# Graph aggregation on one core: broadcast buffers from a pool of their own, and smaller merge credits between the decoding's steps

## Chip, core and metric

One core of a Trainium2 chip. The time is the device time of one launch in microseconds (us). The kernel before was timed three times: 1854.63, 1863.13 and 1864.98 us, median 1863.13. One further execution, of 1856.37 us, was profiled; every row quoted here comes from it. Engines are named as in the profile: PE multiplies matrices (PEld loads its weights), DVE is VectorE, ACT is ScalarE, POOL is GpSimd, SP is SyncE, which only issues transfers here.

## What is computed

A mean over neighbours in a graph of 12,500 nodes with 64 features each and 800,000 edges drawn at random, and two small products:

```
nsum    = segment_sum(x[src], dst, N)      # 800,000 rows of 64 added by destination
h_neigh = nsum * deg_inv[:, None]
out     = x @ w_self + h_neigh @ w_neigh
```

The edges come in no order. The whole difficulty is to add 800,000 gathered rows by destination.

## The kernel before

**From edges to buckets.** Each edge becomes one 32-bit key, in which the destination block (82 nodes per half, two halves to a block, 77 blocks) stands above the source block (128 nodes, 98 blocks), and the places within the blocks stand in the lowest bits. A pair of blocks is a *bucket*, or a column; there are 77 x 98 = 7546. The keys are sorted in 128 partitions, cut by value into three *parts* of 29, 20 and 10 buckets per partition (columns 0 to 3711, 3712 to 6271, and the rest), exchanged between partitions through DRAM, and merged. Each part goes through a first set of merges (16 runs to 1), a row split (`split_rows`, with a store to DRAM and eight gathers back by POOL, line 565), a second set of merges (8 runs to 1), and a *decode*. The merges are tensor_tensor minimum and maximum instructions of VectorE (lines 316, 328, and 362 for the last merge of the first part), with a few copies by ScalarE (line 312).

**The decode of a part** (`decode_buckets`). POOL gathers for every bucket a window of keys around it into `v` (lines 736 and 742). In groups of four buckets VectorE splits the keys (`split`, lines 782 and 784), ScalarE narrows them to bf16 (`narrow`, lines 791, 792, 796), the source places are stored to the DRAM list `sl` (line 794, for the first part by SyncE), and the destination places are turned by PE (`turn`, line 802) into `dlT`. After the last group VectorE searches the margins of all windows for keys that did not fit their bucket, the *leftovers* (`beyond` and `pieces`, lines 831, 834 and 860), in `v` and a scratch tile `e`.

**The tile loop** (`nodes`). Columns are worked in tiles of eight, 950 of them. For each chunk of 28 columns `one_hots` broadcasts the source places from `sl` to all partitions (`slb`, line 933: four transfers of 224 KB on SyncE's queue, three buffers), compares them with the partition number (`ohs`, line 935, VectorE), and compares `dlT` with a row of numbers (`ohd`, line 940, VectorE). The loop keeps 44 columns of one-hots ahead of the tile. PE picks the feature rows out of SBUF with `ohs` (line 966), ScalarE copies them to 16 bit (`xg`, line 976), and PE adds them into the destination blocks with `ohd` (line 1047). After every six destination blocks (73.5 tiles) the sums are multiplied by the weights, scaled and added to the output in DRAM by POOL (line 1123). Leftovers are fetched row by row by POOL (`lx`, line 997) and added with one-hots of their own (lines 1006 and 1015).

**The order of the work** is written out by hand: from `after_sort` on, each engine runs its instructions in the order in which the Python code emits them. In that order the merges of parts 1 and 2 fill VectorE beside the decode of the first part and beside the tile loop. A merge instruction yields a charge in ns (`n2 * n / 0.96 + 125`). Between two decoding steps of the first part `t` is raised by a credit, and merges are emitted until it is used up:

```
for i, k in enumerate(self.decode_buckets(0, self.v, vp, mps)):
    t += 1400 if i < 4 else 2800
    if k < KPRS[0]:
        t = fill(t) if t > 0 else t
```

There are 16 such steps, two to a group; the merges behind the last of them come before the search. In the tile loop each tile gives a credit of `PACE[min(merging, 2)] - self.spent`, where `spent` counts VectorE's other extra work and `merging` is 1 until the second merges of part 1 are through, and then 2 and 3. Part 1's decode begins when its second merges are through, and must end 12 tiles before its first column is due; the same holds for part 2. When part 2's decode is through (`changed`), VectorE takes a share of ScalarE's copies.

**Memory.** Tiles come from pools, which are stacked from the left and from the right end of SBUF. `v`, `e` and the decode's small tiles lie in the pool `va`, the first part's merge buffers in `first_two`. Both are closed after the decode, and the tile loop's pool `fin` is then opened from the right; `slb`, `ohs`, `ohd`, `xg` and the leftovers' tiles are in `fin`. An instruction that writes a tile waits until what lay in the same memory has been read.

Of the kernel before, what the change touches and what calls it, by code (L numbers as in the profile page):

```python
# [13 lines left out]
BF = mybir.dt.bfloat16  # L14
# [34 lines left out]
NSUP = 128 // SUP  # L49
LENA = [l[3:] for l in LENS]  # L50
LENB = [l[4:] for l in LENS]
PACE = (0, 420, 405)
LROW = [l[-1] for l in LENS]
LEAD = 616
EXT = 36
# [318 lines left out]
class Kernel:  # L374
# [549 lines left out]
    def one_hots(self, pool):  # L924


        nc = self.nc
        for c in range(0, NBID, 28):
            n = min(28, NBID - c)
            b = pool.tile([128, 28 * 128], BF, name="slb", bufs=3)[:, :n * 128]  # L930
            src = self.sl[c:c + n]
            for j in range(4):
                nc.sync.dma_start(b[j::4], bass.AP(tensor=src.tensor, offset=src.offset, ap=[[0, 32], [1, n * 128]]))  # L933
            s = pool.tile([128, 28, 128], FH, name="ohs", bufs=3)[:, :n]
            nc.vector.tensor_scalar(s.rearrange("p c s -> p (c s)"), b, self.pidx[:, :1], None, op0=OP.is_equal)  # L935
            d = pool.tile([128, 14, HN, 2], FH, name="ohd", bufs=4)[:, :n // 2]
            at = c % TURN
            wide = [128, n // 2, HN, 2]
            ix = self.dlT[:, at:at + n].rearrange("p (c t) -> p c t", t=2)[:, :, None, :].to_broadcast(wide)
            nc.vector.tensor_tensor(d, self.iota[:, None].to_broadcast(wide), ix, op=OP.is_equal)  # L940
            yield [(s[:, j], d[:, j // 2, :, j % 2]) for j in range(n)]
# [345 lines left out]
    def sums_and_merge(self, es, mps, aps, x, u1, u2, u3, runs, first_two, va, vp, counts, merge):  # L1287
        tc = self.tc

        def fill(t):  # L1290
            while t > 0:
                dt = next(merge, None)
                if dt is None:
                    return 0
                t -= dt
            return t

        while counts:
            fill(1)
            for _ in range(2):  # L1300
                if counts and next(counts, None) is None:
                    counts = None
        fill(BEHIND)
        self.gather_buckets(0, NFIRST, KPRS[0])
        t = 0
        for i, k in enumerate(self.decode_buckets(0, self.v, vp, mps)):
            t += 1400 if i < 4 else 2800
            if k < KPRS[0]:
                t = fill(t) if t > 0 else t
        va.close()  # L1310
        first_two.close()


        self.late = True
        self.fin = fin = es.enter_context(tc.tile_pool(name="fin", bufs=1, side="right"))
        self.left = {}
        self.picked = -9
        self.mps = mps
        self.spent = 0
        side = [[self.leftovers(0), 0]]  # L1320
        chain = None
        part, merging = 0, 1
        work = ExitStack()
        last = None
        t = 0
        home = {1: (u1, x, u1), 2: (u2, u1, u2)}
        todo = [(merge, None)]
        given, checked = 0, False

        def split(part, n):  # L1330
            u, w, pong = home[part]
            for wait in self.split_rows(part, u, w, mps, self.nc.gpsimd):
                yield wait
            todo.append((self.merge_runs(LENB[part], w, pong, SUP), part))

        for n in self.nodes(fin, aps, mps):
            for job in list(side):
                if n >= job[1]:
                    wait = next(job[0], None)
                    if wait is None:  # L1340
                        side.remove(job)
                        if len(self.left) == NP and not checked:
                            checked = True
                            side.append([self.check(fin, mps), 0])
                    else:
                        job[1] = n + wait
            if chain is None and part + 1 < merging:
                part += 1
                vp = work.enter_context(tc.tile_pool(name=f"v{part}", bufs=1))
                chain = self.change(part, vp, mps)  # L1350
                last = None
            if chain:
                if last != "gather" or not n % 2 and self.picked < n - 1:
                    last = next(chain, None)
                    if last is None:
                        assert n < BASE[part] // 8 - 12
                        chain = None
                        self.changed = part == NP - 1
                        work.close()
                        side.append([self.leftovers(part), n + 3])  # L1360
            t += PACE[min(merging, 2)] - self.spent
            self.spent = 0
            while t > 0 and todo:
                dt = next(todo[-1][0], None)
                if dt is not None:
                    t -= dt
                    continue
                rows = todo.pop()[1]
                if rows:
                    self.rows[rows] = home[rows][1]  # L1370
                    merging += 1
                else:
                    given += 1
                    assert given == 1 or merging == 2
                    side.append([split(given, n), n + 6])
                    if given == 1:
                        todo.append((self.merge_runs(LENA[2], u2, u3, NSUP), None))
            if not todo:
                t = min(t, 0)
        assert checked  # L1380
        for job, _ in side:
            for _ in job:
                pass
        assert merging == 3 and part == 2 and not chain
        runs.close()
# [27 lines left out]
```

## Time and profile before

| | |
|---|---|
| timed runs | 1854.63, 1863.13, 1864.98 us |
| profiled execution | 1856.37 us, span 1854.6 us |
| busy over the span | PE 986.6 us, DVE 1718.2, ACT 1116.7, POOL 576.2 |
| last merge round of the first part starts | 685.7 us |
| decode of the first part | 737 to 787 us |
| search for leftovers | 787 to 797 us |
| first one-hot of the tile loop | 803.41 us |
| second merges of part 1 through | 1168 us |
| first merges of part 2 through | 1420 us |
| second merges of part 2 through | 1572 us |

A row of the timeline gives the start, the busy time, the engine, the line, the operation, output and inputs, the number of instructions that were merged into the row and, in brackets, the idle time of the engine before it with what ended it. "SPq" is the time at which SyncE's queue issues a transfer; the transfer itself lands later. A row of a group ends with the number of instructions, their busy time and the mean of one in ns, and the idle time ahead of them. The engines' shares over the whole span say little here, since the sort, the decode and the tile loop have different limits: stretches are read instead.

### The profile page before, as it was taken

Reading aid. Unit: us, or ns where it says so; the run is one execution under the profiler, and the core shown is the slowest. Engines: PE = TensorE matmul, PEld = TensorE weight load, DVE = VectorE, ACT = ScalarE, POOL = GpSimd, SP = SyncE. Lnnn points to the kernel's source line nnn. Section 1 sums busy time; section 2 is a strip of 40 time slices with the busy share of each in tenths; the row PEclk is TensorE's granted clock in tenths of the full one; section 3 lists DMA queues with packets and bytes.
Section 4 is the critical chain, followed back from the end, with each engine's and each line's share of the span. In section 5 each row is a group of like instructions: output and inputs, shape, how many; then the busy total and the mean of one; then the engine's idle time right before and its main releaser. Section 6 shows DMA issues by size and latency. Waiting matters only on the chain.

```text
span 1854.6 us, 54153 instructions
## 1 busy us (share of the span) xinstructions
PE 986.6 (53%) x23413; PEld 851.9 (46%) x23413; DVE 1718.2 (93%) x1718; ACT 1116.7 (60%) x1587; POOL 576.2 (31%) x447
## 2 busy tenths in 40 slices
PE   3046000000000000058979979897898899888996
PEld 1015000000000000057868868776887788777885
DVE  6999999999999999989989999998898799978885
ACT  5263000113001005458979989899999899977885
POOL 2000000055502005404456535473332523532331
PEclk7567555555555555579989999999999999999998
DMA  5207100021002002169978888996889788977894
GB/s 174 54 0 169 39 0 0 38 79 51 18 4 73 10 0 82 47 216 266 274 249 253 251 248 254 296 282 227 264 250 284 234 265 242 326 200 257 274 268 118
DMA packets 176789, 307.79 MB, mean 166 GB/s; under 512 B 127885, under 2 KB 133596, under 8 KB 175772
## 3 DMA queue, kind: packets, MB, share of 16 engines
q1 hardware_dynamic: 98268, 275.58, 44.9%
q0 software_dynamic: 78272, 28.65, 9.6%
q8 instruction: 185, 3.03, 0.7%
q14 instruction: 64, 0.52, 0.1%
HBM read 277.01 MB, written 26.52 MB: 164 GB/s over the span
## 4 chain that ended last, share of the span: by engine, by line
DVE 19%; PE 13%; DMA 11%; issue 10%; SPq 5%; POOL 4%; ACT 4%; DVEq 0%; POOLq 0%; ACTq 0%
DMA slb<-sl 10%; PE ct L966 7%; DVE u L328 7%; PE acc L1047 5%; SPq L933 5%; DVE ohs L935 4%; DVE ohd L940 3%; ACT xg L976 2%; DVE u L362 2%; POOL u L565 1%; POOL lx L997 1%; POOL out L1123 1%; DVE u L316 1%; DMA sl<-l 1%; PE acc L1015 1%
## 5 line engine op out<-in xcount | busy, mean ns | idle before, releaser
L976 ACT ACTIVATE xg<-ct 128x1024 f16<-128x1024 f32 x919 | 862.6, 1074 | 104.4 <-PE ct L966 80.0
L966 PE MATMUL ct<-xh,ohs 128*128 128x128 f16 x7546 | 532.6, 224 | 87.9 <-DVE ohs L935 23.7
L966 PEld LDWEIGHTS <-ohs 128*128 128x128 f16 x7546 | 451.8, 100 | 125.4 <-issue 52.5
L328 DVE TENSOR_TENSOR u<-u 128x1512 f32<-128x1512 f32 (+57 forms) x316 | 425.7, 1362 | 12.9 <-ACT u L312 8.6
L1047 PE MATMUL acc<-ohd,xg 64*128 64x82 f16 x15092 | 395.2, 201 | 47.7 <-ACT xg L976 20.4
L1047 PEld LDWEIGHTS <-xg 64*128 64x128 f16 x15092 | 324.6, 96 | 104.6 <-issue 29.2
L997 POOL DMA_INDIRECT lx<-xt,ls x127 | 232.0, 1826 | 425.6 <-PE acc L1015 352.5
L940 DVE TENSOR_TENSOR ohd<-iota,dlT 128x2296 f16<-128x2296 bf16 x270 | 362.2, 1341 | 0.0
L935 DVE TENSOR_SCALAR ohs<-slb,pidx 128x3584 f16<-128x3584 bf16 x270 | 321.8, 1192 | 40.2 <-DMA slb<-sl 19.0
L509 PE MATMUL stp<-cx,swapa 128*128 128x16 f32 (+1 forms) x12 | 3.1, 335 | 398.0 <-DVE swapa L505 398.0
L260 DVE TENSOR_TENSOR a<-b 128x1040 f32<-128x1040 f32 (+41 forms) x130 | 194.7, 1539 | 3.5 <-DVE b L260 0.5
L260 DVE TENSOR_TENSOR b<-a 128x1040 f32<-128x1040 f32 (+46 forms) x150 | 194.6, 1345 | 3.2 <-ACT a L262 0.4
L538 POOL DMA_INDIRECT u<-d,ixa x48 | 72.5, 1511 | 390.8 <-ACT junka L526 335.4
L509 PEld LDWEIGHTS stp<-cx,swapa 128*128 128x128 f32 x12 | 2.6, 271 | 398.5 <-DVE swapa L505 398.5
L312 ACT ACTIVATE u<-u 128x256 f32<-128x256 f32 (+14 forms) x60 | 33.0, 618 | 170.6 <-DVE u L316 134.8
L1123 POOL DMA_DIRECT2D out<-o x27 | 99.1, 3800 | 103.1 <-ACT o L1117 89.8
L802 PE MATMUL tr<-idb,l 128*128 128x128 bf16 x59 | 7.6, 263 | 188.9 <-ACT l L796 188.9
L262 ACT ACTIVATE b<-a 128x2 f32<-128x2 f32 (+31 forms) x41 | 15.9, 402 | 127.1 <-DVE a L260 120.4
L802 PEld LDWEIGHTS <-l 128*128 128x128 bf16 x59 | 4.3, 114 | 191.2 <-ACT l L796 190.8
L316 DVE TENSOR_TENSOR u<-u 128x2016 f32<-128x2016 f32 (+11 forms) x40 | 61.9, 1563 | 16.2 <-DMA u<-da,ixb 8.8
L262 ACT ACTIVATE a<-b 128x1 f32<-128x1 f32 (+24 forms) x34 | 8.6, 259 | 105.4 <-DVE b L260 99.9
L565 POOL DMA_INDIRECT u<-da,ixb x24 | 36.9, 1539 | 88.6 <-ACT ixb L513 85.0
(158 smaller groups left out, 839.4 us busy)
## 6 DMA issues: line engine op xcount, KB each, us to landing
slb<-sl SPq DMA_DIRECT2D x1076, 224.0 KB
xt<-xh SPq DMA_DIRECT2D x1, 3136.0 KB
out<-o POOLq DMA_DIRECT2D x25, 123.0 KB
own<-os SPq DMA_DIRECT2D x12, 256.0 KB
out<-os SPq DMA_DIRECT2D x12, 256.0 KB
rd<-dst SPq DMA_DIRECT2D x5, 512.0 KB
rs<-src SPq DMA_DIRECT2D x5, 512.0 KB
lx<-xt,ls POOLq DMA_INDIRECT x127
```

Of the source, the lines that this page charges most:

```text
L260: nc.vector.tensor_tensor(view(dst, lo + sh, [[st, g], [1, l]]), x, y, op=op)
L316: nc.vector.tensor_tensor(at(oth, to, n), x, y, op=op)
L328: nc.vector.tensor_tensor(to, at(cur, ln + lo, n), at(cur, lo + k, n), op=op)
L538: nc.gpsimd.indirect_dma_start(out=u[:, i * w:(i + 1) * w], out_offset=None, in_=src, in_offset=bass.IndirectOffsetOnAxis(ap=self.start[pa ...
L933: nc.sync.dma_start(b[j::4], bass.AP(tensor=src.tensor, offset=src.offset, ap=[[0, 32], [1, n * 128]]))
L935: nc.vector.tensor_scalar(s.rearrange("p c s -> p (c s)"), b, self.pidx[:, :1], None, op0=OP.is_equal)
L940: nc.vector.tensor_tensor(d, self.iota[:, None].to_broadcast(wide), ix, op=OP.is_equal)
L966: nc.tensor.matmul(ct[:, i * 128:(i + 1) * 128], cols[i][0], self.xh[:, (b0 + i) % NB].rearrange("p a f -> p (a f)"), start=True, stop=True)
L976: nc.scalar.activation(xg[:, :cnt * 128], ct[:, :cnt * 128], AF.Copy)
L997: nc.gpsimd.indirect_dma_start(out=x, out_offset=None, in_=self.xt, in_offset=bass.IndirectOffsetOnAxis(ap=self.left[p][1][:, c:c + 1].bit ...
L1047: nc.tensor.matmul(acc[h][:, db % OCT * HN:(db % OCT + 1) * HN], xg[r, i * 128:(i + 1) * 128], d[r], start=db % OCT == 0 and sb == 0, stop ...
L1123: nc.gpsimd.dma_start(out, o[:n, at], accum_op=OP.add)
```

## The change

`slb` is allocated from a pool `wait`, which is opened from the right before the first part's decode is emitted, while `va` and `first_two` are still open; it stays open to the end. The tile loop's pool is opened further in by as much as `wait` takes. The code that issues the broadcasts stays at its place in the order. From the fifth decoding step on the credit is 1700 instead of 2800. The tile loop's credits are 450 instead of 420 while part 1 is merged, and 420 instead of 405 after that.

```
-PACE = (0, 420, 405)
+PACE = (0, 450, 420)
...
-            b = pool.tile([128, 28 * 128], BF, name="slb", bufs=3)[:, :n * 128]
+            b = self.wait.tile([128, 28 * 128], BF, name="slb", bufs=3)[:, :n * 128]
...
         fill(BEHIND)
         self.gather_buckets(0, NFIRST, KPRS[0])
+        self.wait = es.enter_context(tc.tile_pool(name="wait", bufs=1, side="right"))
         t = 0
         for i, k in enumerate(self.decode_buckets(0, self.v, vp, mps)):
-            t += 1400 if i < 4 else 2800
+            t += 1400 if i < 4 else 1700
```

## The prediction

> **What bounds the kernel now.** I read the busy time of each engine over stretches cut at the merge milestones first, since the share of the whole span hides the stages. Columns: stretch and length, then PE, PEld, DVE, ACT and POOL busy (instructions), granted clock, DMA share, GB/s.
>
> ```profile
> 737.00:787.00 50.00, 4.54 (x29) 2.52 (x29) 48.14 (x56) 22.25 (x43) 25.84 (x32) 0.50 0.19 53
> 787.00:803.00 16.00, 0.00 (x0) 0.00 (x0) 10.05 (x26) 0.00 (x0) 1.75 (x3) 0.50 0.26 79
> 803.00:905.00 102.00, 88.88 (x2249) 79.10 (x2249) 98.36 (x132) 89.66 (x103) 35.80 (x20) 0.95 0.89 261
> 905.00:953.00 48.00, 39.03 (x947) 34.38 (x946) 39.28 (x43) 43.23 (x65) 26.78 (x24) 0.89 0.92 293
> 953.00:1168.00 215.00, 189.28 (x4778) 167.48 (x4779) 213.26 (x199) 193.83 (x234) 101.31 (x36) 0.96 0.84 248
> 1168.00:1282.00 114.00, 95.66 (x2375) 82.62 (x2374) 103.72 (x148) 108.02 (x155) 60.98 (x44) 0.98 0.88 281
> 1282.00:1420.00 138.00, 128.21 (x3309) 114.21 (x3305) 131.41 (x185) 131.42 (x167) 49.16 (x25) 0.98 0.83 252
> 1420.00:1572.00 152.00, 134.63 (x3349) 119.39 (x3350) 136.85 (x147) 139.60 (x181) 57.19 (x38) 0.94 0.84 254
> ```
>
> Three things are to be seen. VectorE alone carries the decode of the first part (48.14 of 50 us); then comes a hole of 16 us in which it works 10.05; then the tile loop, where it is busy 350.9 of 365 us until 1168, the end of part 1's second merge. After 1168 PE, VectorE and ScalarE are near each other and none is full.
>
> Next the timeline of VectorE and SyncE at the hole.
>
> ```profile
> 746.94 6.23 DVE L328 TENSOR_TENSOR u<-u 128x1344 f32<-128x1344 f32 x4
> ...
> 780.83 0.35 DVE L782 SCALAR_TENSOR_TENSOR w<-v,c 128x64 int32<-128x64 int32 x2
> ...
> 781.36 4.36 DVE L328 TENSOR_TENSOR u<-u 128x1262 f32<-128x1262 f32 x3
> 785.75 1.48 DVE L316 TENSOR_TENSOR u<-u 128x1264 f32<-128x1264 f32 x1
> 787.15 1.95 DVE L831 TENSOR_TENSOR e<-v,c 128x1728 int32<-128x1728 int32 x1
> ...
> 796.14 1.04 DVE L860 MAX8 top<-e 128x8 f32<-128x72 f32 x5
> 797.32 52.63 SPq L933 DMA_DIRECT2D slb<-sl  x64
> ...
> 803.41 1.15 DVE L935 TENSOR_SCALAR ohs<-slb,pidx 128x3584 f16<-128x3584 bf16 x1 [6.22 <-DMA slb<-sl]
> ```
>
> And the waits, of the queue SyncE over 737 to 803 and of VectorE and PE over 803 to 1168 (total, times, longest):
>
> ```profile
> SPq L933 <- DVE top L860: 13.6, 1, 13.6
> ...
> DVE ohs L935 <- DMA slb<-sl: 9.0, 5, 6.2
> DVE u L316 <- DMA u<-da,ixb: 7.3, 1, 7.3
> ...
> PE ct L966 <- DVE ohs L935: 18.3, 11, 8.2
> ```
>
> The first broadcast waits 13.6 us for the last search for leftovers (it lies in memory that the search reads), leaves at 797.32 and has landed at 803.41; VectorE stands 6.2 us for it. In the tile loop it is VectorE that others wait for, with one stall of its own of 7.3 us.
>
> **Part 1, memory of their own.** The first broadcast now needs only the last store of the list (L794). With nothing else changed it would leave some 14 us earlier and land before the search ends. That removes 6.2 us. No instruction is added; the three buffers only move out of the pool opened later, and the 12 issues of the first three chunks now run beside the search, where SyncE has nothing else queued. SyncE is in order: what waits behind the first issue is only further broadcasts.
>
> **Part 2, less merging in the decode.** The steps' credits fall from 4x1400+12x2800 = 39,200 to 4x1400+12x1700 = 26,000. A merge instruction is charged its elements/0.96+125; adding the plan's charges step by step gives 28 instructions before and 19 after (2, 2, 2, 3, 2, 3, 2, 3 behind the eight splits instead of 2, 2, 4, 3, 5, 4, 4, 4). The groups of 737 to 787 give the price, and that the 28 or 29 are there:
>
> ```profile
> L328 DVE TENSOR_TENSOR u<-u 128x1344 f32<-128x1344 f32 (+16 forms) x26 | 37.5, 1463 | 1.5 <-ACT u L312 1.1
> ...
> L316 DVE TENSOR_TENSOR u<-u 128x1352 f32<-128x1352 f32 (+1 forms) x3 | 4.5, 1534 | 0.1
> ```
>
> Nine of these at 1.45 us are 13.0 us. Laid out with the durations of the timeline, the third split ends at 747.0, the later ones start at 750.1, 755.9, 760.1, 765.6 and 769.6, and the search starts at 774.5 and ends at 784.5. So the first one-hot comes 18.9 us before 803.41: 6.2 of stall and 12.7 of merging (0.3 less than 13.0, since pieces overlap).
>
> That holds if nothing else is late next. The splits read windows that POOL gathers, and the broadcast reads the store:
>
> ```profile
> 762.03 0.95 POOL L736 DMA_INDIRECT v<-d,ix  x1 [0.16 <-issue]
> 763.33 1.72 POOL L736 DMA_INDIRECT v<-d,ix  x1 [0.16 <-issue]
> ...
> 738.26 3.29 DMA v<-d,ix
> ...
> 1252.60 5.29 DMA sl<-l
> ```
>
> The last two gathers start at 762.03 and 763.33; at 3.29 us to landing (the piece in the chain of waits) they are there at 765.3 and 766.6, against splits at 765.6 and 769.6: a tie for the seventh group, up to 1 us lost. The last store is issued about 1.3 us after its split, at 770.9. Its landing is bounded above by the 5.29 us of a larger store under load, below by the 3.29 of the gather: 774.2 to 776.2. Then 6.1 us (797.32 to 803.41) as now: 780.3 to 782.3, so 2.2 to 4.2 us before VectorE asks. If that cover went, the cost is what the chain store-broadcast overruns, at most the 6.2 of today.
>
> **Part 3, where the nine merges go.** They land in the tile loop, at 13.0 us of VectorE work. The credit per tile goes from 420 to 450 while part 1 is merged, later from 405 to 420. The same adding of charges over tiles puts the end of part 1's second merge at tile 340 instead of 329 (the trace has 328 tiles up to 1168, below), the end of part 2's first at 550 instead of 552, and the point from which VectorE shares the copies at 738 instead of 744. The groups of 803 to 1168:
>
> ```profile
> L940 DVE TENSOR_TENSOR ohd<-iota,dlT 128x2296 f16<-128x2296 bf16 x95 | 127.6, 1343 | 0.0
> L935 DVE TENSOR_SCALAR ohs<-slb,pidx 128x3584 f16<-128x3584 bf16 x95 | 114.3, 1203 | 12.0 <-DMA slb<-sl 9.0 <-PE ct L966 1.3 <-PE acc L1047 1.0
> ...
> L976 ACT ACTIVATE xg<-ct 128x1024 f16<-128x1024 f32 x328 | 305.8, 1081 | 53.6 <-PE ct L966 30.7 <-DMA slb<-sl 22.4
> ```
>
> A tile costs VectorE (1343+1203)/3.5 = 727 ns of one-hots (28 columns a chunk, 8 a tile). VectorE being full up to 1168, the nine merges are paid there: 13.0 us. Against this, 11 tiles move from behind part 1's decode to ahead of it. There (1282 to 1420, about 138 tiles by 3309 PE records at 24 a tile) a tile takes 1.0 us, ahead they cost 0.73: 11x0.28 = 3.1 back. The higher credit after that costs between 0 (VectorE has 6.6 of 138 and 15.2 of 152 us free) and 15 ns on each of 349 tiles, 5.2 us; I take 1, nearer the free end, as those rows show. The six tiles at the end change nothing I can size; the stage costs about 1 us a tile on either side. So 13.0 - 3.1 + 1 = 10.9 are paid back.
>
> **Sum.** 18.9 - 10.9 = 8.0 us gained. The profiled execution took 1856.4 (span 1854.6 and 1.8 around it), so 1848.4 on its own scale. It is a low one of the four shown (1854.6, 1856.4, 1863.1, 1865.0; mean 1859.8). I forecast from the mean: **1852**.
>
> **Rivals.** A, the merging is hidden. The chain of waits over 1000 to 1050, by line:
>
> ```profile
> by line: PE ct L966 47.3%; PE acc L1047 36.2%; issue 7.4%; ACT xg L976 4.5%; PE acc L1015 3.5%; ACT u L312 1.9%; ACTq L976 0.0%
> ```
>
> For A: there the chain runs over PE, busy 189.28 of the 215 us around it; were PE the bound there, VectorE's extra work would cost nothing and up to the whole 18.9 would stay: 1841. Against: VectorE is idle only 1.7 of those 215 us, and PE waits for it, not the reverse.
>
> B, the broadcast is not early: its new memory or the store's landing holds it. Then 6.2 of the 18.9 fall out, 1.8 are left: 1858. For: the slack is only 2.2 us. Against: the wait named is the search alone.
>
> C, slower: the stall at part 1's row split grows. Its place:
>
> ```profile
> 931.11 1.24 POOL L565 DMA_INDIRECT u<-da,ixb  x1 [9.89 <-ACT ixb L513]
> ...
> 938.01 1.14 DVE L935 TENSOR_SCALAR ohs<-slb,pidx 128x3584 f16<-128x3584 bf16 x1
> ...
> 938.20 5.24 POOL L565 DMA_INDIRECT u<-da,ixb  x1 [0.16 <-issue]
> ...
> 952.74 1.69 DVE L316 TENSOR_TENSOR u<-u 128x1472 f32<-128x1472 f32 x1 [7.25 <-DMA u<-da,ixb]
> ```
>
> Eight gathers, counted out by tile, must land before the next merge, which stands in VectorE's order ahead of all later one-hots. From the first gather to the merge are 21.6 us, of which 7.25 are stall. In the changed kernel part 1's first merge ends at tile 117 instead of 93 (the same adding of charges), so this comes 24 tiles later, among other POOL work. If the whole 21.6 showed, 14.4 more are lost: 1859.8 - 8.0 + 14.4 = 1866. It decides from a stall of 15.3 us (no gain left). Against: POOL has fewer result stores near the new place (the sums of a group of nodes end every 73.5 tiles), so it may as well shrink by up to 7.
>
> One rule bears on C, and only on its chance. The gather at 938.20 took 5.24 us while VectorE ran one-hots and two merges. The Trainium skill ("SBUF — State Buffer", Who interferes with whom) says that VectorE in a two-port mode locks GpSimd out of the port it writes descriptors through, and infers that a two-input tensor_tensor does not. By that, more merges between the one-hots would shorten these gathers and the stall; by the row, which spans both kinds, they would not. I leave the chance as the rows have it.
>
> **How the numbers follow.** Forecast, gain of 4 to 12 (1848 to 1856): 0.50. A, gain of 12 to 19: 0.21. B: 0.13. C: 0.16. The timings of before lie up to 5 us from their mean, and the ends of the unknown costs are 0.7 (18.9 - 13.0 - 5.2) and 18.9 us of gain; C's price extends the upper end. Range 1838 to 1867; the forecast's own, with half that scatter, is 1845 to 1859. About 0.5% (9.3 us) is what can be told from no change. Faster by more: all of A and nearly half of the forecast's cases, with the scatter, 0.43. Same: the rest of it, B and the milder half of C, 0.44. Slower: 0.13, from C.
>
> **What would show it.** First one-hot at about 784.5 (end of the first part's decode at 774.5) with no wait for a broadcast before it; first broadcast before the first large search ends; 19 merges among the decode's steps; part 1's second merge, which ended near 1168, ending near 1168 - 18.9 + 13.0 + 11x0.73 = 1170, though 11 tiles further on, and VectorE full up to there. Wrong if VectorE is idle in the loop (A), if the 6 us wait is still there (B), or if the stall of 7.3 has doubled (C).

## The result, and the profile after

The changed kernel takes **1842.41 us** in the median (1837.49 to 1847.04), the kernel before on the same chip 1857.43 (1852.45 to 1866.61). The ratio is 0.9901 with a 95% interval of 0.9877 to 0.9925. That is a gain of 18.4 us by the ratio, between 13.9 and 22.8; the two medians alone lie 15.0 us apart. It is faster by more than the 0.5% that can be told. The time lies inside the predicted range of 1838 to 1867, but below the forecast's own 1845 to 1859. It lies next to the 1841 that rival A gave. The profiled execution took 1839.47 us, its span is 1837.8.

Ahead of the tile loop all went as laid out. From the timeline of the changed kernel, VectorE and SyncE's queue:

```profile
765.60 0.76 DVE L782 SCALAR_TENSOR_TENSOR w<-v,c 128x256 int32<-128x256 int32 x2 [0.59 <-DMA v<-d,ix]
...
769.56 0.36 DVE L782 SCALAR_TENSOR_TENSOR w<-v,c 128x64 int32<-128x64 int32 x2
...
771.36 7.49 SPq L933 DMA_DIRECT2D slb<-sl  x12
...
774.38 1.95 DVE L831 TENSOR_TENSOR e<-v,c 128x1728 int32<-128x1728 int32 x1
...
783.38 1.04 DVE L860 MAX8 top<-e 128x8 f32<-128x72 f32 x5
784.61 1.52 DVE L935 TENSOR_SCALAR ohs<-slb,pidx 128x3584 f16<-128x3584 bf16 x1 [0.19 <-issue]
...
965.10 1.69 DVE L316 TENSOR_TENSOR u<-u 128x1472 f32<-128x1472 f32 x1 [7.86 <-DMA lx<-xt,ls]
```

The twelve broadcasts of the first three chunks leave from 771.36 on, the first of them ahead of the search. The first one-hot starts right behind the search, at 784.61, and waits for no transfer. It comes 18.8 us earlier than the 803.41 of before. The groups of 737 to 774.3 count the merges among the decode's steps:

```profile
L328 DVE TENSOR_TENSOR u<-u 128x1344 f32<-128x1344 f32 (+10 forms) x17 | 24.4, 1448 | 1.3 <-ACT u L312 1.1
...
L316 DVE TENSOR_TENSOR u<-u 128x1352 f32<-128x1352 f32 x2 | 3.0, 1557 | 0.0
```

These are 19 instead of 28 (the 29 in the rows of before hold one that had begun ahead of the first split and ended at 737.07). The waits of the changed kernel, of VectorE and PE from the first one-hot to the end of part 1's second merge (784.6 to 1162) and of SyncE's queue over 737 to 803 (total, times, longest):

```profile
DVE u L316 <- DMA lx<-xt,ls: 7.9, 1, 7.9
DVE ohs L935 <- DMA slb<-sl: 1.5, 2, 1.2
...
PE ct L966 <- DVE ohs L935: 30.5, 15, 14.9
...
SPq L933 <- DVE ohs L935: 9.7, 4, 7.2
```

SyncE no longer waits for the search. The one long stall of VectorE in that stretch, at part 1's row split, is 7.9 us (7.3 before). Busy time by stretch, cut at the changed kernel's own milestones:

```profile
737.00:774.00 37.00, 4.54 (x29) 2.51 (x29) 34.79 (x45) 22.24 (x43) 26.63 (x32) 0.50 0.29 82
774.00:784.60 10.60, 0.00 (x0) 0.00 (x0) 10.28 (x26) 0.00 (x0) 0.00 (x0) 0.50 0.67 221
784.60:913.00 128.40, 113.11 (x2847) 101.07 (x2847) 127.31 (x157) 114.75 (x133) 54.62 (x27) 0.95 0.86 254
913.00:962.00 49.00, 42.64 (x1032) 37.54 (x1034) 42.99 (x48) 45.20 (x68) 23.41 (x23) 0.93 0.85 278
962.00:1162.00 200.00, 173.40 (x4385) 152.95 (x4384) 196.87 (x185) 178.96 (x215) 90.48 (x35) 0.96 0.84 246
```

VectorE is nearly full until 1162, as it was until 1168: 367.2 of 377.4 us (127.31 + 42.99 + 196.87). So most of the nine merges did land on a full VectorE. And yet the loop as a whole is hardly longer. One row for each kernel, from its first one-hot to its end, first before and then after:

```profile
803.41:1854.57 1051.16, 911.61 (x23139) 808.42 (x23139) 957.14 (x1145) 930.12 (x1187) 423.14 (x241) 0.96 0.84 255
```

```profile
784.61:1837.76 1053.15, 914.03 (x23139) 810.51 (x23139) 972.50 (x1155) 929.78 (x1186) 420.26 (x244) 0.96 0.84 253
```

VectorE has 15.4 us more work in the loop (957.14 to 972.50), of which nine more merges are 13.2 and one more copy 1.2, and the loop is 2.0 us longer. VectorE's idle time fell from 94.0 to 80.7 us. That is the surprise: the engine that others wait for took on 15 us and lost 13 us of its own waiting.

Where that happened is seen by chunk number, not by time, since both kernels make the same 270 pairs of one-hots. The start of a chunk's `ohs` in the changed kernel lies ahead of the same chunk in the kernel before by 18.8 us at chunk 0, 15.7 at chunk 90, 19.2 at chunk 120, 15.8 at chunk 150, 14.6 at chunks 180 and 210, 20.1 at chunk 240 and 17.3 at the last. So 3.1 us are paid until chunk 90, won back up to the end of part 1's decode (chunk 120), paid again, won back behind part 2's decode, and in part lost once more at the end. These are differences of one execution of each kernel.

### The profile page after: what moved, and what is told of

Read it like the earlier page. It is cut to its first block, busy times and chain, and to the rows that moved or that the text cites. A ratio compares the mean times of both kernels' runs of the same rounds, so it can differ in the third digit from the quotient of the medians.

```text
span 1837.8 us, 54140 instructions
## 1 busy us (share of the span) xinstructions
PE 996.6 (54%) x23413; PEld 861.1 (47%) x23413; DVE 1720.6 (94%) x1719; ACT 1115.8 (61%) x1586; POOL 572.3 (31%) x447
## 4 chain that ended last, share of the span: by engine, by line
DVE 15%; DMA 14%; PE 9%; issue 8%; SPq 5%; ACT 4%; POOL 3%; DVEq 0%; POOLq 0%; ACTq 0%
DMA slb<-sl 13%; DVE ohs L935 5%; PE ct L966 5%; DVE ohd L940 4%; SPq L933 4%; PE acc L1047 3%; DVE u L328 3%; ACT xg L976 3%; POOL u L565 1%; DMA lx<-xt,ls 1%; DVE u L316 1%; DVE ohl L1006 1%; POOL lx L997 0%; POOL out L1123 0%; PE po L1114 0%
## 5 line engine op out<-in xcount | busy, mean ns | idle before, releaser
L328 DVE TENSOR_TENSOR u<-u 128x1512 f32<-128x1512 f32 (+58 forms) x316 | 426.0, 1362 | 12.2 <-ACT u L312 7.9
L316 DVE TENSOR_TENSOR u<-u 128x2016 f32<-128x2016 f32 (+11 forms) x40 | 61.8, 1561 | 18.3 <-DMA u<-da,ixb 10.1
```

The lines of the kernel that those rows point to most:

```text
L316: nc.vector.tensor_tensor(at(oth, to, n), x, y, op=op)
L328: nc.vector.tensor_tensor(to, at(cur, ln + lo, n), at(cur, lo + k, n), op=op)
```

## The experiments

The kernel before took 1857.43 us where the result above was taken (chip a), 1866.19 on chip b, 1858.25 on chip c and 1867.60 on chip d. Chips b, c and d are three; which chip a was isn't on record, and it may be one of them. Only kernels on one chip are compared directly, and each has its ratio against the kernel before on its own chip.

**One part at a time (chip b).** The first is the changed kernel with the merge credits of before:

```diff
-PACE = (0, 450, 420)
+PACE = (0, 420, 405)
...
-            t += 1400 if i < 4 else 1700
+            t += 1400 if i < 4 else 2800
```

> The broadcasts' own memory alone, credits as before. Both theories take the 6.2 us stall of VectorE before the first one-hot away and nothing else: a ratio to the kernel before of 0.9967. Theory 1 (the prediction's: merging that is moved into the tile loop is paid there) then has the credits worth 2 us, and this kernel within 2 us of their remainder to the changed one if the whole gain was the pool's; theory 2 (rival A: the moved merging slips into idle time of VectorE) has the credits worth about 10 us more than this kernel shows.

Measured: 1856.52 us, ratio 0.9959 (0.9937 to 0.9980), a gain of 7.7 us (3.7 to 11.8). Its timeline:

```profile
797.56 1.52 DVE L935 TENSOR_SCALAR ohs<-slb,pidx 128x3584 f16<-128x3584 bf16 x1 [0.19 <-issue]
```

The stall is gone, the first one-hot comes 5.9 us earlier, and the whole of it stays. The second is the kernel before with the new credits, so `slb` stays in the loop's pool:

```diff
-PACE = (0, 420, 405)
+PACE = (0, 450, 420)
...
-            t += 1400 if i < 4 else 2800
+            t += 1400 if i < 4 else 1700
```

> The smaller decoding credit and the larger tile credits, broadcasts in the old memory. The wait of the first broadcast for the last search stays, some 6 us. Theory 1: ratio 0.998 to 1.000 (12.7 gained in the decode, 10.9 paid back). Theory 2: 0.993 to 0.995 (12.7 gained, 0 to 3 paid back).

Measured: 1861.54 us, 0.9973 (0.9955 to 0.9992), a gain of 5.0 us (1.5 to 8.4). Its timeline, and its queue's wait:

```profile
791.24 1.15 DVE L935 TENSOR_SCALAR ohs<-slb,pidx 128x3584 f16<-128x3584 bf16 x1 [5.92 <-DMA slb<-sl]
```

```profile
SPq L933 <- DVE top L860: 12.1, 1, 12.1
```

The first one-hot comes 12.2 us earlier, with the stall in its old place. Of these 12.2 some 7.2 (3.8 to 10.7) are paid back in the loop. On this chip, then, the nine merges are paid about halfway, which is not what the changed kernel shows on chip a. The traces of these two can't say where: the profiled execution of the first lies 7.8 us above its median, that of the second 7.0 below.

**Is VectorE's work free in the loop? (chip b.)** Twenty `ohd` of the changed kernel are made twice, either in the first 95 chunks, while VectorE is full, or in chunks 102 to 202:

```diff
+            if c // 28 in range(2, 92, 9) or c // 28 in range(6, 96, 9):
+                nc.vector.tensor_tensor(d, self.iota[:, None].to_broadcast(wide), ix, op=OP.is_equal)
```

> The changed kernel with 20 of the first 95 destination one-hots made twice in place (the same values), which is 20 x 1.26 = 25 us more VectorE work and nothing else, up to part 1's decode. Theory 1 (VectorE full there): 20 to 25 us slower than the changed kernel, a ratio to before of about 1.002 to 1.004. Theory 2: under 8 us slower, about 0.990 to 0.994.

> The same 20 doubled one-hots (25 us of VectorE work) spread over chunks 102 to 202, from part 1's decode to part 2's. Theory 1 as in the prediction (none of the engines full there): 5 to 15 us slower than the changed kernel, about 0.993 to 0.998. Theory 2: 0 to 8 us slower, 0.990 to 0.994. If this stage takes the work for less than the early one, idle time is where the payback went.

Measured: 1878.71 us, 1.0063 (1.0038 to 1.0088) early, and 1869.41, 1.0019 (0.9997 to 1.0041) late. The changed kernel itself was not run on this chip. Against the 0.990 that it has elsewhere, the 28 us of extra work cost about 30 us early and 22 late; against the product of the two parts measured on this chip (0.9959 x 0.9973 = 0.9932) they cost 24 and 16. Either way VectorE's work is not free, not even late, where VectorE had idle time. Rival A's reason falls with this.

**The changed kernel again, and the credits against each other (chip c).**

> The changed kernel itself, timed beside the following ones on their chip, so that the parts can be added up. If the two parts add (0.9959 of the pool, 0.9973 of the credits), 0.993; by its first timing 0.990. Theory 1 (moved merging is paid in the loop, 10.9 of 13 us) gives 0.9957, theory 2 (slips into idle time) 0.990.

The changed kernel without any edit: 1840.25 us, 0.9899 (0.9866 to 0.9931). The gain of chip a stands. Next the changed kernel with the old credit between the decode's steps, but the larger credit per tile:

```diff
-            t += 1400 if i < 4 else 1700
+            t += 1400 if i < 4 else 2800
```

> The pool and the larger tile credits, but the decode's credit as before: no merging is moved behind the decode, the tile loop only does its merges some 25 tiles sooner. Theory 1: VectorE's work is the same and it is the bound, so as the pool alone: 0.996. Theory 2 (work sooner lets idle time later be used less): 0.997 to 0.999. If the larger tile credit is itself the gain, 0.992 to 0.994.

Measured: 1862.34 us, 1.0009 (0.9986 to 1.0031). It is 20.4 us slower than the changed kernel on the same chip by the ratios (0.0110 x 1858). Its first one-hot comes at 798.41, which is 13.8 us later, and another 6.7 us are lost in the loop: VectorE has 7.6 us less to do there than in the changed kernel, and still the loop is longer. Its row over the loop:

```profile
798.41:1860.89 1062.48, 912.54 (x23139) 809.72 (x23139) 963.28 (x1150) 927.76 (x1182) 437.03 (x244) 0.95 0.83 251
```

VectorE idles 99.2 us in it. With both credits high the merges are through sooner: in the traces the last one stands in chunk 188 rather than 197, some 31 tiles earlier. Without less merging in the decode the larger credit per tile does not pay. Whether it pays beside it was not run: no kernel has the smaller credit in the decode with the old credits per tile.

The control: the kernel before with ten `ohd` of the first 100 chunks made twice, as much VectorE work as the nine merges, at about the same place, with the plan of before:

```diff
+            if c // 28 in range(2, 102, 10):
+                nc.vector.tensor_tensor(d, self.iota[:, None].to_broadcast(wide), ix, op=OP.is_equal)
```

> The kernel before with ten of its first 100 destination one-hots made twice in place: about 13 us of VectorE work added to the tile loop, as much as the nine moved merges bring, and nothing else. It is the price of the payback by itself. Theory 1: 10.9 to 14 us slower, 1.006 to 1.0075. Theory 2: 0 to 5 us, 1.000 to 1.0027.

Measured: 1871.34 us, 1.0070 (1.0048 to 1.0093), a loss of 13.0 us (8.9 to 17.3) for 14.3 us of work. It is paid in full. With the changed kernel beside it on one chip, nearly the same VectorE work in the loop (971.4 and 970.8 us) and both profiled executions within 1.5 us of their medians, this is the cleanest pair of the study. Besides the plan it differs in the memory of `slb`, which by itself changed the loop by -1.8 us (-5.9 to 2.1) on chip b. Windows of the control, for chunks 105 to 135, 135 to 210, 210 to 240, and the whole loop, then the same of the changed kernel:

```profile
1216.50:1340.80 124.30, 105.12 (x2602) 91.78 (x2599) 110.60 (x177) 116.33 (x166) 60.81 (x40) 0.96 0.81 242
1340.80:1623.60 282.80, 252.18 (x6396) 222.83 (x6396) 263.73 (x300) 263.26 (x340) 118.79 (x68) 0.96 0.88 267
1623.60:1745.40 121.80, 103.18 (x2576) 92.86 (x2577) 102.76 (x150) 97.83 (x129) 43.20 (x26) 0.94 0.81 238
...
803.31:1869.80 1066.49, 912.67 (x23139) 808.81 (x23139) 971.44 (x1155) 931.73 (x1187) 418.33 (x241) 0.95 0.83 251
```

```profile
1192.10:1313.00 120.90, 107.23 (x2575) 93.60 (x2570) 112.67 (x184) 115.99 (x168) 65.45 (x43) 0.94 0.84 257
1313.00:1596.90 283.90, 256.02 (x6424) 226.96 (x6421) 263.40 (x303) 264.94 (x344) 114.41 (x69) 0.95 0.87 266
1596.90:1714.10 117.20, 102.51 (x2652) 91.88 (x2651) 104.59 (x147) 98.63 (x128) 40.57 (x26) 0.98 0.83 246
...
784.64:1837.02 1052.38, 916.47 (x23139) 813.47 (x23139) 970.84 (x1155) 929.63 (x1186) 427.58 (x244) 0.95 0.84 253
```

Length less DVE is VectorE's idle time: 95.1 us in the control, 81.5 in the changed kernel. Of the 13.5 us between them, 5.5 lie in chunks 105 to 135, around part 1's decode (13.7 against 8.2), and 6.4 in chunks 210 to 240, behind part 2's decode (19.0 against 12.6). Between these the idle time is nearly the same (19.1 and 20.5). What VectorE waited for over the loop (without the wait ahead of the first one-hot): the control first, where the two helper lines stand two lines lower, then the changed kernel:

```profile
DVE xg L976 <- PE ct L968: 19.7, 15, 4.1
DVE ohs L935 <- PE ct L968: 19.7, 14, 5.2
DVE ohs L935 <- DMA slb<-sl: 14.0, 10, 3.2
```

```profile
DVE xg L974 <- PE ct L966: 16.9, 12, 6.0
DVE ohs L935 <- PE ct L966: 15.9, 16, 2.4
...
DVE ohs L935 <- DMA slb<-sl: 8.0, 7, 2.5
```

Waits for PE's picked rows fell from 39.4 to 32.8 us, waits for the broadcasts from 14.0 to 8.0, and the decodes' own waits (the splits for ScalarE's narrowed places `l`, the search for leftovers for a transfer, `many`) from 6.9 to 1.0. The stalls at the two row splits rose from 11.5 to 16.4. Then chunks 105 to 135 alone, around part 1's decode, in the same order:

```profile
DVE w L782 <- ACT l L792: 5.0, 2, 2.5
DVE ohs L935 <- DMA slb<-sl: 4.0, 3, 2.3
DVE ohs L935 <- PE ct L968: 4.0, 2, 3.2
```

```profile
DVE ohs L935 <- PE ct L966: 6.4, 6, 2.4
DVE w L782 <- ACT l L792: 1.0, 1, 1.0
```

So there it was not PE: the waits for ScalarE's `l` and for the broadcasts went from 9.0 to 1.0, and those for PE rose. On chip a the same two went from 7.6 us to none.

In chunks 210 to 240 something else differs too. The granted clock is 0.94 in the control and 0.98 in the changed kernel: the trace has PE at half clock for 13.7 of 121.8 us in the one and for 6.8 of 117.2 in the other, and on chip a the kernels before and after have the same 13.7 and 6.8. Over all fourteen traces VectorE idles 9.1 to 16.1 us in these chunks where the half clock lasts 6.8 us (five traces), 13.3 to 19.2 at 10.2 us (three), and 13.3 to 22.2 at 13.7 us and more (six). Whether the plan moved the half clock or the half clock made the idle time was not tested. Around part 1's decode there is no such link: on chip a 6.8 us in both kernels.

The last of this chip slows the merges of part 1 and speeds up those of part 2:

```diff
-PACE = (0, 450, 420)
+PACE = (0, 430, 450)
```

> The changed kernel with tile credits of 430 and 450 in place of 450 and 420: the merging of part 1 runs 13 tiles longer, part 2's is done 5 tiles sooner. Theory 1: VectorE's work is the same, within 2 us of the changed kernel. Theory 2: the early stage is relieved of 7 us of work, which later idle time takes: 3 to 6 us faster than the changed kernel.

Measured: 1839.47 us, 0.9897 (0.9862 to 0.9932), the same as the changed kernel.

**Does it hang on where the decodes begin? (chip d.)** By the plan part 1's second merges end 11 tiles later in the changed kernel, and part 2's 7 tiles earlier. The first experiment puts part 1's decode of the kernel before to tile 341, the second holds part 2's decode of the changed kernel back to tile 697:

```diff
-            if chain is None and part + 1 < merging:
+            if chain is None and part + 1 < merging and n >= 341:
```

```diff
-            if chain is None and part + 1 < merging:
+            if chain is None and part + 1 < merging and (part == 0 or n >= 697):
```

> The kernel before, with part 1's decode held back to tile 341, where it begins in the changed kernel, instead of tile 330; the merges keep their places. VectorE's work is the same. Theory 1 (only VectorE's work counts): 1.000. Theory 3 (the payback went into idle time that VectorE has where part 1's decode meets the sums of a group of nodes; 13.5 us of idle time over chunks 105 to 135 in the kernel before, 7.5 in the changed one): 4 to 7 us faster, 0.9965 to 0.998, with the idle time of that stretch at 7 to 9 us.

> The changed kernel, with part 2's decode held back to tile 697 as in the kernel before, instead of 690. Same work. Theory 1: as the changed kernel, 0.990. Theory 3 (the rest of the payback went into idle time after part 2's decode; 19 us over chunks 210 to 240 before, 11 in the changed kernel): 5 to 9 us slower than the changed kernel, 0.993 to 0.995.

The first: 1867.04 us, 1.0004 (0.9977 to 1.0030). No gain; the later start of part 1's decode is not the reason by itself, or brings 4.3 us at most. The second: 1858.04 us, 0.9962 (0.9932 to 0.9992), a gain of 7.1 us where the changed kernel has 18.4 on chip a.

Then the changed kernel with ten `ohd` of the first 100 chunks left out (the chunk before's are used again, so its sums are not the reference's), and with slower merges in part 2:

```diff
+            again = c // 28 in range(2, 102, 10)
+            if not again:
+                whole = pool.tile([128, 14, HN, 2], FH, name="ohd", bufs=4)
+            d = whole[:, :n // 2]
...
+            if not again:
+                nc.vector.tensor_tensor(d, self.iota[:, None].to_broadcast(wide), ix, op=OP.is_equal)
```

```diff
-PACE = (0, 450, 420)
+PACE = (0, 450, 395)
```

> The changed kernel with ten of its first 100 destination one-hots left out: the chunk before's are used again, so the sums of those chunks are not the reference's. 13 us of VectorE work less in the tile loop, as much as the nine moved merges. Theory 1 (VectorE is the bound on the way down too): 11 to 14 us faster than the changed kernel, 0.983. Theory 2 (the last 13 us of work were hidden): 0 to 4 us faster, 0.988 to 0.990.

> The changed kernel with a second tile credit of 395 instead of 420: part 2's decode ends near tile 760 instead of 738, VectorE's work is the same. If merging that ends one tile later saves 0.28 us (a tile's 1.0 us without merging against 0.73 of one-hots, which would explain the 9 us that the larger credits cost without the smaller decoding credit): 6 us faster than the changed kernel, 0.987. Theory 3: decided by where part 2's decode meets the groups, -5 to +8 us.

With ten fewer: 1846.17 us, 0.9895 (0.9856 to 0.9934). With slower merges: 1853.96 us, 0.9918 (0.9894 to 0.9943); the 6 us more that "a tile later saves 0.28 us" would have brought are not there. Its splits of part 2's decode come six chunks later than those of the kernel with the held decode (from chunk 214 on against 208), and it keeps 8.2 us more, though the intervals overlap. Chunks 210 to 240 of the kernel with the held decode and of the one with ten fewer:

```profile
1607.70:1730.00 122.30, 103.96 (x2599) 92.78 (x2599) 103.11 (x150) 99.94 (x132) 41.48 (x27) 0.96 0.80 239
```

```profile
1598.90:1720.00 121.10, 104.81 (x2605) 94.18 (x2606) 105.83 (x146) 97.66 (x129) 41.00 (x27) 0.94 0.81 237
```

VectorE idles 19.2 us with the held decode and 15.3 without (the half clock lasts 10.2 us in both), where the control on chip c had 19.0 and the changed kernel 12.6. So the hold gives back some 4 us of idle time in the stretch behind part 2's decode. That is a part of its loss at most: the ten one-hots that the other kernel lacks could explain the 12.5 us between the two by themselves, at one for one. The changed kernel would have had to run beside them, and did not.

**All of them together.** "Earlier" is the first one-hot against 803.41, "gain" is by the ratio, "paid" is "earlier" less "gain" with the interval of the ratio, and "work" is VectorE's busy time in the loop against 957.1, from each profiled execution.

| kernel | chip | earlier | gain | paid in the loop | work added |
|---|---|---|---|---|---|
| changed | a | 18.8 | 18.4 | 0.4 (-4.0 to 4.9) | 15.4 |
| changed again | c | 18.8 | 18.8 | 0.0 (-6.1 to 5.9) | 13.7 |
| later pace | c | 18.4 | 19.1 | -0.7 (-7.2 to 5.8) | 13.2 |
| old credit in the decode | c | 5.0 | -1.7 | 6.7 (2.4 to 10.8) | 6.1 |
| before, ten twice | c | 0.1 | -13.0 | 13.1 (9.0 to 17.4) | 14.3 |
| own memory only | b | 5.9 | 7.7 | -1.8 (-5.9 to 2.1) | -0.8 |
| credits only | b | 12.2 | 5.0 | 7.2 (3.8 to 10.7) | 14.4 |
| changed, twenty twice early | b | 17.9 | -11.8 | 29.7 (25.0 to 34.4) | 41.0 |
| changed, twenty twice late | b | 18.9 | -3.5 | 22.4 (18.3 to 26.6) | 43.1 |
| before, decode later | d | 0.0 | -0.7 | 0.7 (-4.3 to 5.6) | 1.6 |
| second decode later | d | 18.3 | 7.1 | 11.2 (5.6 to 16.8) | 12.6 |
| ten reused | d | 18.1 | 19.6 | -1.5 (-8.8 to 5.8) | 1.1 |
| slower merges in part 2 | d | 17.3 | 15.3 | 2.0 (-2.5 to 6.7) | 10.4 |

On chips a and c the three kernels that merge less in the decode and more per tile pay nothing that can be told (6 us at most) for 13 to 15 us of work; the two that add work to another plan pay all of it. On chips b and d the picture is mixed. No version on chip c can be told to be faster than the changed kernel; on b and d it was not run.

## Why the prediction was right in part, and where it failed

**Memory of their own: right.** The stall of 6.2 us went, the broadcasts left at 771.36 (laid out: behind a store issued at 770.9), and the kernel with this part alone kept all of it. Rival B is refuted.

**Less merging in the decode: right.** 19 merges, the first one-hot at 784.61 (784.5). The last two splits start at 765.60 and 769.56 (765.6 and 769.6). The feared tie of the seventh group with POOL's gather was a wait of 0.59 us.

**Where the nine merges go: this step failed.** The text said "VectorE being full up to 1168, the nine merges are paid there: 13.0 us", took 3.1 back and added 1. The work and the place were right: nine merges more in the loop took 13.2 us, VectorE is nearly full to 1162, and the second merges of part 1 end there, against 1170 predicted. The price was not: by chunk 90 the lead had shrunk by 3.1 us, for 8.5 us more merging, and by the end of part 1's decode all of it was back. The sum of 10.9 should have been 0.4, between -4.0 and 4.9, and the forecast's 8.0 us of gain became 18.4.

The reason is not that VectorE's work was free, as rival A had it. The control paid 13.1 us for 14.3 on the same chip as the changed kernel, and the doubled one-hots paid 16 to 30 us for 28. What the step left out is VectorE's idle time, 94.0 us in the loop, some 80 of them behind the full stage. I treated it as a fixed cost per tile (a tile costs 0.73 us ahead of part 1's decode and 1.0 behind), so that only the 11 moved tiles could change it. It is not fixed: it is made of waits, and it was 13.4 us shorter in the changed kernel, with nine merges more in the loop. Of the 13.5 us between the control and the changed kernel on one chip, 11.9 lie at the two decodes.

**What of that is shown, and what is not.** Shown, on chips a and c: the work is there, the time for it is not, and VectorE idles less at the two decodes, though where the idle time lies rests on one execution of each kernel. Shown on chip c: the smaller credit in the decode is needed (with the larger credit per tile alone the kernel is 20.4 us slower), and the same amount of work under the plan of before is paid. Refuted, to within 4.3 us: that the later start of part 1's decode does it by itself.

At part 1's decode the idle time that went was waits for ScalarE's `l` and for the broadcasts; why the new plan ends them is open.

Only argued: that the earlier end of part 2's decode, from which VectorE shares ScalarE's copies, does the second half. Holding it back brought 4 us of idle time, on a chip where the changed kernel was not run; the kernel with slower merges, whose decode of part 2 comes later still, speaks against it; and the half clock, which lasts 6.8 us there instead of 13.7, is a rival that no run separates.

On chip d the kernel with slower merges keeps 15.3 us although VectorE idles 15.4 and 22.2 us at the two decodes, as in the near twin of the kernel before (15.2 and 22.0), so less idle time there is not seen in every kernel that gains. Open too: whether the changed kernel gains 18 us on chips like b and d, where the credits alone paid 7.2 us back; the two parts' gains there add up to 12.7.

**Rival C: refuted.** The stall at the row split was 7.86 us, not doubled. From the first gather to the merge passed 20.7 us (21.6 before). The profile puts the end of the stall down to a transfer of leftover rows (`lx`), which POOL issues among the gathers; the merge began 4.6 us after the last gather was issued, against 2.5 before. The eight gathers took 0.95 to 2.56 us each, where one had taken 5.24, with five merges among three pairs of one-hots instead of four. The Trainium skill ("SBUF — State Buffer", Who interferes with whom) infers that a tensor_tensor leaves free the write interface that GpSimd needs for its descriptors; by that, denser merges would shorten the gathers. These traces don't settle it: in the control, with merges as dense as before, the eight took 0.95 to 1.87 us, and in the changed kernel two gathers of leftover rows ahead of the eight took 5.26 and 4.23. The stall did not shrink with the gathers either, so nothing of the time hung on it.

**The range.** That it held is luck: its upper bound of gain (18.9, all merging free) was carried over from a rival whose reason was wrong. The chance of 0.21 for a gain of 12 to 19 was too low for an idle time of 94 us that I had no account of.

## What to carry to other kernels

"Work moved into a full stage is paid there" holds for the stage, not for the whole loop: sum the busiest engine's idle time over all of the loop first, by stretch, and ask what each wait hangs on, since a new plan of the work that fills an engine's gaps can change its waits by as much as the work itself weighs (13.4 us of idle time against 13.2 of merges here). Compare two traces at the same unit of work (the chunk number here), not at the same time, and put as much extra work of another kind into the old kernel as a control: here that told that the same amount of work is paid under the plan of before. Compare the granted clock of the stretches before a difference in idle time is put down to the plan. Where the effect is under 1%, the unchanged candidate has to be on every chip that an experiment is run on; that it wasn't on chips b and d is why questions stay open here.

## What the hardware showed that was not expected

**The same kernel differs by half a per cent between chips, and PE shows where.** The kernel before took 1857 and 1858 us on chips a and c (which may be one), 1866 and 1868 on b and d. Chips b, c and d were each used in one stretch of time, so that chip and time can't be told apart. Its near twin on chip d (part 1's decode held back, no effect) has this row over the loop, against 1051.16 us and 911.61 of PE for the kernel before on chip a:

```profile
803.40:1864.36 1060.96, 926.46 (x23139) 816.74 (x23139) 958.78 (x1145) 931.92 (x1187) 420.23 (x241) 0.95 0.84 252
```

VectorE's and ScalarE's busy times agree within 1.8 us (957.14 and 930.12 before); the same 23139 matmuls take 14.9 us more. All eight kernels on chips b and d have 924 to 932 us of PE, all six on a and c 912 to 916. The granted clock does not part them: it is 0.95 to 0.96 on a and c and 0.94 to 0.95 on b and d, and at 0.95 PE took 916.5 us in the changed kernel on chip c and 926.5 in the row above. What differs in the waits is PE standing for nothing that the profile shows ("issue"), from the start of the loop to the end; the kernel before on chip a, then the one with own memory only on chip b:

```profile
PE acc L1047 <- issue: 11.4, 15, 1.8
PE ct L966 <- issue: 10.1, 13, 1.9
```

```profile
PE acc L1047 <- issue: 19.8, 33, 1.6
PE ct L966 <- issue: 19.0, 32, 1.7
```

It is 21.5 us in 28 pieces against 38.8 in 65. The longest cluster of that kernel stands in its timeline:

```profile
1448.38 0.40 PE L966 MATMUL ct<-xh,ohs 128*128 128x128 f16 x4 [0.39 <-issue]
1449.14 0.38 PE L966 MATMUL ct<-xh,ohs 128*128 128x128 f16 x4 [0.36 <-issue]
...
1450.57 0.49 PE L966 MATMUL ct<-xh,ohs 128*128 128x128 f16 x4 [1.04 <-issue]
...
1453.44 0.33 PE L1047 MATMUL acc<-ohd,xg 64*128 64x82 f16 x4 [0.95 <-issue]
...
1455.01 1.15 DVE L935 TENSOR_SCALAR ohs<-slb,pidx 128x3584 f16<-128x3584 bf16 x1 [8.66 <-remote]
```

For some nine us PE takes its matmuls four at a time with a gap of up to 1 us before each four, for nothing that the profile shows, and VectorE stands 8.66 us behind it, released by what the profile only calls "remote". Such waits stand in all eight kernels on chips b and d (2.9 to 11.1 us in the loop) and in none of the six on a and c. It looks like PE being short of instructions, while POOL's gathers of the row split run beside it; that is a guess, and no run here tested it. The transfers of the profile's instruction queue, 16 KB each, lend it no support: by the trace's records the one within the cluster took 0.93 us, those ahead of it and behind it 1.04 and 0.93, and over the loop they took 0.95 us in the median in this kernel and in the one before. In these traces, then, PE's time is not the same price on every chip.
